# Storing an attention unit's output and softmax sums in five parts by heads in place of one store of 128 rows

## The chip, the cores and the metric

The kernel runs on one core of one Trainium2 chip. The metric is the device time of one execution in microseconds (us); lower is better. The engines are named as in the profile: PE is TensorE (matmuls; PEld its weight loads), DVE is VectorE, ACT is ScalarE, POOL is GpSimd, SP is SyncE. SPq and ACTq are the queues on which SP and ScalarE issue transfers (DMAs).

## The reference

The input x has 2048 rows of 640. It is normalized per row to xn, and the result is x + A(xn) + B(xn):

- A is attention with 32 heads of width 20 and a sliding window of 256: scores = q k^T / sqrt(20), masked so that a row sees itself and the 255 rows before it, softmax, times V, then times wo (640 x 640).
- B is a gated feed-forward of width 1728: gelu(xn w_gate) * (xn w_up), then times w_down.

## The kernel before, in words

Tokens are handled in NC = 4 chunks of C = 512. float32 products are made from a high and a low part (three matmuls each). The work has four stretches: normalization, transposes and the first projections; the attention loop, whose matmuls are interleaved with the remaining projections and a part of the gate and up products as filler; the remaining gate and up products; and the down and output projections.

**Units.** The attention loop (`attention`) runs over NU = 32 units. Unit u = 4 g + c is the group g of four heads and the chunk c. A unit has NS = 14 slots; in each slot some actions are emitted, and then RATE / NS filler matmuls (`pull_fill`). `defer(n, fn)` puts an action n slots later; `tick` runs what is due.

For a unit, in the order of time:

- `load_stack` (line 473, DMA at L482) brings the queries and keys of unit u + 3 from DRAM (`qd`, `kd`) into `qs` (three buffers) and `ks` (four buffers): six transfers each, of 20, 40 or 60 rows of 2 KB. The keys are asked for in slot KSLOT = 9, the queries in slot 12. They may start only when the matmuls that read the old content (L572) are done.
- `max_pair` (matmuls L507 into `ps_m`, row maxima by VectorE at L517) runs about one and a half units ahead of the exponentials. The first pair of unit u + 3 is emitted in slot 5 of unit u + 1.
- `max_end` (line 531) turns the maxima by a matmul (L534), copies them to `mr` (L536, ScalarE), and ScalarE itself issues the transfer `qs<-mr` (L537), which adds two rows to the queries. It is an entry in ScalarE's queue like any other, ahead of the activations behind it.
- `exp_piece` makes the scores (L572 into `ps_e`, two banks) and the exponentials (L574, ScalarE) into `P`; `clear` (L587, L590) sets masked ends to zero on POOL.
- `av_unit` (line 593), at the start of the next unit, multiplies P by V (L615 into two banks `ps_o`). V has a column of ones at each head's end, so that row 20 of each head's 32 rows holds the softmax sum. ScalarE copies one bank to `ob` (L621) and the other over a piece of P (L622); `join` (L625, three slots later) adds the second to the first on POOL; `store` (L628, five slots later) writes `ob` to DRAM. `ob` has one buffer: the next unit's copy at L621 waits for the store to have landed.

In `ob`, partition 32 j + d holds head 4 g + j: rows d = 0 to 19 are the output, row 20 is the sum, rows 21 to 31 are not used. In DRAM, `od[c]` (line 89) has 32 x 32 rows of 512, row 32 d + h for head h; `sd[c]` is the view of its rows 640 to 671, the sums. The later readers are L1085 (the sums), L1097 to L1108 (the outputs are divided by the sums and written back) and L1166 and L1169 (the outputs as operands of the last projection); they use rows 0 to 671 only.

**Who sets the order.** In the attention loop the order of PE, ACT, DVE and POOL is that of the program (`manual_schedule`, MANUAL and Pool). SP's order is not written out: the compiler's planner puts SP's transfers in order by when they become ready in its own model of time, and by program order among those. SP also issues the stores of projected queries and keys (`save_qk`, L268, from `pt`, made by POOL at L259), weight loads (L234, L637, L294), partial sums of x (L755, from `tx`, POOL) and hidden activations (L689).

Of the kernel before, what the change touches and what calls it, by code (L numbers as in the profile page):

```python
# [9 lines left out]
F32 = mybir.dt.float32  # L10
# [7 lines left out]
S, D, H, DH = 2048, 640, 32, 20  # L18
DF = 1728
C = 512  # L20
NC = S // C
# [46 lines left out]
def block_kernel(ctx, tc, x, wqk, wv, wgu, wdo, wdl, out):  # L68
    nc = tc.nc

    const = ctx.enter_context(tc.tile_pool(name="const", bufs=1))
    dram = ctx.enter_context(tc.tile_pool(name="dram", bufs=1, space=DRAM))
# [13 lines left out]

    qd = [dram.tile([NG, 3, 4 * DH, C], BF, name=f"qd{c}") for c in range(NC)]
    kd = [dram.tile([NG, 3, 4 * DH, C], BF, name=f"kd{c}") for c in range(NC)]
    od = [dram.tile([32 * H, C], F32, name=f"od{c}") for c in range(NC)]
    sd = [t[D:D + H] for t in od]  # L90
    td = [{i: dram.tile([128, 2, C], F32, name=f"td{p}{i}") for i in (1, 2, 3, 4)} for p in range(NC // 2)]
    wtd = [dram.tile([128, 4, HD], F32, name=f"wtd{q}") if q not in OWN else None for q in range(NQD)]
    rd = [dram.tile([H, C], F32, name=f"rd{c}") for c in range(NC)]
# [125 lines left out]
    def defer(n, fn, *a):  # L219
        if now[0] is None:  # L220
            fn(*a)
        else:
            at(now[0] + n, fn, *a)
# [315 lines left out]
    def pieces(c):  # L539
        b = 4 * c  # L540
        X = [(b, 0, 0, 384)] + ([(b - 2, 384, 0, 128)] if c else [])
        Y = [(b + 1, 0, 128, 384), (b + 3, 384, 384, 128)]
        Z = ([(b - 1, 0, 0, 256)] if c else []) + [(b + 2, 256, 256, 256)]
        return X, Z, Y
# [48 lines left out]
    def av_unit(u):  # L593
        g, c = divmod(u, NC)
        v = vtiles[g]
        os = [psx.tile([128, C], F32, name="ps_o", tag="ex") for _ in range(2)]
        place = {kb - 4 * c: (pts[u, bi], col, q0) for bi, bank in enumerate(pieces(c)) for kb, col, q0, n in bank}

        def half(d, r):
            i = 2 * d + r  # L600
            return d, r, max(0, 64 * i), min(C, 64 * i + 320)

        steps_ = [((0, 0), (0, 1)), ((2, 0), (-1, 1)), ((-1, 0), (2, 1)), ((1, 0), (1, 1)),
                  ((3, 0), (-2, 1)), ((-2, 0), (3, 1))]
        todo = [half(*x) for pair in steps_ for x in pair if x[0] in place]
        begun_, left = set(), [sum(t[1] == r for t in todo) for r in range(2)]
        for d, r, qa, qb in todo:
            pt, col, q0 = place[d]
            kb = 4 * c + d
            assert (id(v), kb) in done, (u, kb)  # L610
            left[r] -= 1
            rows = slice(64 * r, 64 * r + 64)
            for j in range(4):
                w0_ = kb * 84 + 21 * j
                nc.tensor.matmul(os[r][32 * j:32 * j + 32, qa:qb], v[rows, w0_:w0_ + 32],  # L615
                                 pt[rows, j, col + qa - q0:col + qb - q0], start=r not in begun_,
                                 stop=not left[r], skip_group_check=True, tile_position=(64 * r, 32 * j))
            begun_.add(r)
        ob, oc = ap.tile([128, C], F32, name="ob", tag="ob", bufs=1), pts[u, 2][:, 0]
        lo = 0 if c else 64  # L620
        nc.scalar.activation(ob, os[0], AF.Copy)  # L621
        nc.scalar.activation(oc[:, lo:], os[1][:, lo:], AF.Copy)  # L622

        def join():
            nc.gpsimd.tensor_tensor(out=ob[:, lo:], in0=ob[:, lo:], in1=oc[:, lo:], op=OP.add)  # L625

        def store():
            nc.sync.dma_start(od[c].rearrange("(d h) t -> h d t", h=H)[4 * g:4 * g + 4], ob)  # L628

        defer(3, join)  # L630
        defer(5, store)

    def load_gu(f):
# [892 lines left out]
```

## Time and profile before

| What | us |
|---|---|
| Time of three runs: median, lowest, highest | 1047.0, 1046.81, 1047.27 |
| The profiled execution's own time | 1046.35 |
| Its span, first to last instruction | 1044.6 |
| PE, DVE, ACT, POOL busy | 1034.0, 741.1, 527.6, 385.9 |
| First and last issue of the store at L628 | 106.4, 548.2 |
| DMA traffic | 161.60 MB in 102276 packets |

The profile is of one execution; its times count from the start of the span. A row of a timeline has the start, the length, the engine, the line, the operation, and out<-in tiles with a count; in brackets stands the idle time before it and what ended that. A row of the chain has start, length and what. "DMA od<-ob" in the chain is the time from a transfer's issue to its landing. A row of the waits has who waited for whom, the total, how often, and the longest. A row of a tile's instructions has min/median/max in ns, and first and last start in us.

### The profile page before, as it was taken

The numbers are of one execution on the slowest core, as the hardware profiler recorded it, in microseconds if no ns is written. First come the engines' busy times: TensorE is split into PE (matmuls) and PEld (weight loads), VectorE is DVE, ScalarE is ACT, GpSimd is POOL, SyncE is SP. The second block draws the span as 40 slices with busy tenths as digits, with TensorE's granted clock in tenths as the row PEclk, the third lists the DMA queues.
The fourth block names the chain that finished last, engine by engine and source line by source line (L and its number), as shares of the span: only waits on it lengthen the run. The fifth ranks groups of instructions, "written<-read, shape, count | busy, mean of one in ns | idle before, by whom it ended". The sixth has DMA issues, their size and how long they took to land.

```text
span 1044.6 us, 25328 instructions
## 1 busy us (share of the span) xinstructions
PE 1034.0 (99%) x9393; PEld 834.9 (80%) x9393; DVE 741.1 (71%) x2018; ACT 527.6 (51%) x1120; POOL 385.9 (37%) x623
## 2 busy tenths in 40 slices
PE   9999999999999999999999999999999999999998
PEld 8887666666787666666678888888888999999998
DVE  7755666676656576777736788775556888888887
ACT  4534767667666666666676232223224554433332
POOL 5122778888666787667470111101110000000000
PEclk9999999999999999999999999999999999999999
DMA  5552356655533464434225575663217874433333
GB/s 211 179 162 78 115 169 175 183 170 163 160 105 107 131 177 145 139 106 154 64 85 197 177 251 206 253 244 111 78 56 254 267 248 137 137 126 121 119 121 106
DMA packets 102276, 161.60 MB, mean 155 GB/s; under 512 B 12892, under 2 KB 53980, under 8 KB 102152
## 3 DMA queue, kind: packets, MB, share of 16 engines
q1 hardware_dynamic: 99768, 153.82, 45.9%
q10 hardware_dynamic: 2384, 6.16, 1.7%
q8 instruction: 74, 1.21, 0.5%
q14 instruction: 50, 0.41, 0.1%
HBM read 101.78 MB, written 57.80 MB: 153 GB/s over the span
## 4 chain that ended last, share of the span: by engine, by line
PE 89%; DVE 4%; POOL 2%; DMA 2%; issue 1%; ACT 1%; SPq 0%; DVEq 0%; POOLq 0%; ACTq 0%
PE ps_g L970 23%; PE ps L1242 23%; PE ps_d L108 18%; PE ps_e L572 7%; PE ps_v L108 7%; PE ps_o L615 5%; PE ps_m L507 4%; DVE junk L517 2%; PE ps_g L108 1%; DMA od<-ob 1%; PE ps_d L356 1%; POOL tx L751 0%; PE ps_t L185 0%; DMA qs<-qd 0%; ACT P L574 0%
## 5 line engine op out<-in xcount | busy, mean ns | idle before, releaser
L517 DVE CUSTOM_DVE_ANT_0 junk<-ps_m,mask 128x320 bf16<-128x320 f32 (+2 forms) x512 | 242.5, 474 | 130.5 <-PE ps_m L507 72.7
L574 ACT ACTIVATE P<-ps_e 128x512 f32<-128x512 f32 (+2 forms) x384 | 198.6, 571 | 68.5 <-PE ps_e L572 67.8
L1242 PE MATMUL ps<-wb,at 128*128 128x320 f32 x999 | 155.9, 309 | 0.0
L1242 PEld LDWEIGHTS ps<-wb,at 128*128 128x128 f32 x999 | 148.9, 188 | 0.2
L587 POOL TENSOR_SCALAR_AFFINE_SELECT P<-P 128x256 f32<-128x256 f32 (+1 forms) x192 | 95.2, 498 | 72.5 <-ACT P L574 69.0
L572 PE MATMUL ps_e<-qs,ks 124*128 124x128 bf16 (+2 forms) x704 | 118.6, 278 | 0.5 <-ACT P L574 0.3
L108 PE MATMUL ps_d<-xh,wqh 128*128 128x512 f32 x310 | 99.0, 422 | 0.2 <-ACT xh L193 0.2
L108 PE MATMUL ps_d<-xl,wqh 128*128 128x512 f32 x310 | 98.5, 421 | 0.0
L108 PE MATMUL ps_d<-xh,wql 128*128 128x512 f32 x310 | 97.6, 418 | 0.0
L101 POOL TENSOR_TENSOR wql<-wr,wqh 128x640 fp32r<-128x640 f32 x12 | 19.2, 1607 | 195.4 <-PE ps_g L970 150.8
L572 PEld LDWEIGHTS <-ks 124*128 124x128 bf16 x704 | 49.5, 98 | 49.8 <-issue 35.6
L1242 PE MATMUL ps<-wt,at 128*128 128x320 f32 x552 | 88.9, 309 | 0.0
L1242 PEld LDWEIGHTS ps<-wt,at 128*128 128x128 f32 x552 | 82.9, 188 | 0.1
L590 POOL TENSOR_SCALAR_AFFINE_SELECT P<-P 128x512 f32<-128x512 f32 (+1 forms) x144 | 76.9, 542 | 16.3 <-ACT P L574 16.3
L1196 ACT ACTIVATE at<-ss 128x512 fp32r<-128x512 f32 x59 | 37.2, 631 | 82.4 <-DVE ss L1075 82.4
L615 PE MATMUL ps_o<-P,v 64*32 64x320 f32 (+4 forms) x2816 | 74.2, 347 | 0.0
L259 POOL TENSOR_TENSOR pt<-r,pt 128x512 bf16<-128x512 f32 x40 | 46.8, 1171 | 67.4 <-ACT pt L255 67.4
L507 PE MATMUL ps_m<-ks,qs 60*64 60x320 bf16 (+3 forms) x1472 | 65.4, 260 | 4.0 <-DVE mx L517 1.5
L615 PEld LDWEIGHTS ps_o<-P,v 64*32 64x32 f32 x2816 | 50.8, 106 | 21.5 <-issue 0.9
L507 PEld LDWEIGHTS <-qs 60*64 60x64 bf16 x1472 | 29.5, 105 | 44.5 <-issue 37.7
L108 PEld LDWEIGHTS ps_d<-xh,wqh 128*128 128x128 f32 x310 | 56.0, 189 | 10.5 <-issue 1.6
L108 PEld LDWEIGHTS ps_d<-xh,wql 128*128 128x128 f32 x310 | 56.0, 189 | 10.2 <-issue 1.1
(195 smaller groups left out, 1966.6 us busy)
## 6 DMA issues: line engine op xcount, KB each, us to landing
hd<-he SPq DMA_DIRECT2D x50, 256.0 KB
hr<-hd SPq DMA_DIRECT2D x48, 256.0 KB
wr<-wgu SPq DMA_DIRECT2D x27, 320.0 KB
od<-ob SPq DMA_DIRECT2D x32, 256.0 KB
qs<-qd SPq DMA_DIRECT2D x64, 120.0 KB
ks<-kd SPq DMA_DIRECT2D x64, 120.0 KB
xi<-x SPq DMA_DIRECT2D x16, 320.0 KB
qs<-qd SPq DMA_DIRECT2D x64, 80.0 KB
```

The source lines that it names most:

```text
L108: nc.tensor.matmul(ps, a(k), b(k), start=n == 0, stop=n == 3 * nk - 1)
L259: nc.gpsimd.tensor_tensor(out=pt[:, l, :], in0=r, in1=pt[:, 1, :], op=OP.subtract)
L507: nc.tensor.matmul(ps[64 * h:64 * h + 64, col:col + w], q[rows, j, q0:q0 + 64], ks_, start=True, stop=True, tile_position=(64 * r, 64 * h))
L517: nc.vector.tensor_tensor_reduce(out=junk[:, 0:n], in0=ps[:, 320 - n:320], in1=mask[:, 320 - n:320], scale=1.0, scalar=NEG, op0=OP.add, op ...
L572: nc.tensor.matmul(ps[:, col:col + n], k[0:QROWS, j, kc:kc + 128], q[0:QROWS, j, q0:q0 + n], start=True, stop=True)
L574: nc.scalar.activation(pt[:, j, lo:hi], ps[:, lo:hi], AF.Exp, scale=SCALE)
L587: nc.gpsimd.affine_select(out=a, in_=a, pattern=[[0, n], [1, 128]], compare_op=OP.is_ge, fill=0.0, base=0, channel_multiplier=-1)
L590: nc.gpsimd.affine_select(out=a, in_=a, pattern=[[0, n], [-1, 128]], compare_op=OP.is_ge, fill=0.0, base=-1, channel_multiplier=1)
L615: nc.tensor.matmul(os[r][32 * j:32 * j + 32, qa:qb], v[rows, w0_:w0_ + 32], pt[rows, j, col + qa - q0:col + qb - q0], start=r not in begun ...
L970: nc.tensor.matmul(ps, i, j, start=first and n == 0, stop=n == len(work) - 1, skip_group_check=True)
L1196: nc.scalar.activation(hi[:, 3:7], s, AF.Copy)
L1242: nc.tensor.matmul(ps[bank][:, 0:HD], *work[bank][j], start=bank not in begun, stop=final[p, bank] == n and j == len(work[bank]) - 1, skip ...
```

## The change

`od[c]` shrinks from 1024 to 640 rows (the unused rows go), and the sums get a tensor of their own, `sd[c]`, of 32 rows. `store` writes, for each of the four heads, 20 rows of 512 floats (40 KB), and then the four rows of sums (partitions 20, 52, 84 and 116; 8 KB). So a unit has five transfers with 168 KB in all, in place of one with 256 KB. The readers stay as they are.

```diff
-    od = [dram.tile([32 * H, C], F32, name=f"od{c}") for c in range(NC)]
-    sd = [t[D:D + H] for t in od]
+    od = [dram.tile([D, C], F32, name=f"od{c}") for c in range(NC)]
+    sd = [dram.tile([H, C], F32, name=f"sd{c}") for c in range(NC)]
...
         def store():
-            nc.sync.dma_start(od[c].rearrange("(d h) t -> h d t", h=H)[4 * g:4 * g + 4], ob)
+            for j in range(4):
+                nc.sync.dma_start(od[c].rearrange("(d h) t -> h d t", h=H)[4 * g + j], ob[32 * j:32 * j + DH, :])
+            nc.sync.dma_start(sd[c][4 * g:4 * g + 4, :], ob[DH::32, :])
```

## The prediction

> **What bounds the kernel now.** I read the page's first and fourth parts first, then the stretches, then the waits of TensorE and of the DMA queue, then the rows of single units.
>
> ```profile
> span 1044.6 us, 25328 instructions
> PE 1034.0 (99%) x9393; PEld 834.9 (80%) x9393; DVE 741.1 (71%) x2018; ACT 527.6 (51%) x1120; POOL 385.9 (37%) x623
> PE 89%; DVE 4%; POOL 2%; DMA 2%; issue 1%; ACT 1%; SPq 0%; DVEq 0%; POOLq 0%; ACTq 0%
> ```
>
> TensorE is busy for 1034.0 of 1044.6 us and makes up 89% of the chain that ended last. A change to a store can therefore gain only where TensorE now stands still, and costs only where it makes TensorE stand still. The store L628 runs from 106.4 to 548.2 us (its row is below), so I cut the span there; the columns are the length, then PE, PEld, DVE, ACT and POOL busy, the clock, the DMA share and GB/s.
>
> ```profile
> 104.00:300.00 196.00, 193.89 (x2565) 131.29 (x2561) 129.95 (x487) 133.50 (x289) 155.99 (x262) 1.00 0.54 159
> 300.00:546.00 246.00, 244.31 (x3304) 167.61 (x3302) 159.61 (x580) 162.66 (x356) 168.38 (x287) 1.00 0.40 120
> ```
>
> In these stretches TensorE stands idle for 196.00 - 193.89 = 2.1 us and 246.00 - 244.31 = 1.7 us. So 3.8 us is the most that the visible idle time could give back, and the granted clock is 1.00 throughout. Who waits for what there:
>
> ```profile
> SPq L482 <- DMA od<-ob: 26.3, 16, 3.4
> SPq L268 <- DMA od<-ob: 10.4, 3, 3.9
> ...
> PEld L507 <- DMA qs<-qd: 2.2, 5, 0.7
> ...
> PE ps_m L507 <- DMA qs<-qd: 0.9, 3, 0.5
> ```
>
> Columns: total, times, longest. The store's landing holds up the DMA queue of SyncE (SP) for 26.3 + 10.4 = 36.7 us; TensorE's own waits on the loads behind it are small, 0.9 us, with 2.2 us more on its weight loads, which partly lie under matmuls. Why the landing holds a queue is seen in one unit. The first two rows are of the chain, the others of the timelines of SP and ACT.
>
> ```profile
> 138.53 7.20 DMA od<-ob
> 145.75 2.92 DMA ks<-kd
> ```
>
> ```profile
> 138.53 0.52 SPq L628 DMA_DIRECT2D od<-ob  x1
> 139.10 0.47 SPq L234 DMA_DIRECT2D wr<-wqk  x1
> 139.67 6.39 SPq L482 DMA_DIRECT2D ks<-kd  x6
> 146.60 1.03 SPq L482 DMA_DIRECT2D qs<-qd  x3
> 147.74 2.11 SPq L268 DMA_DIRECT2D qd<-pt  x3
> 149.96 1.06 SPq L482 DMA_DIRECT2D qs<-qd  x3
> 151.12 1.33 SPq L268 DMA_DIRECT2D kd<-pt  x3
> 152.55 0.50 SPq L755 DMA_DIRECT2D td<-tx  x1
> ```
>
> ```profile
> 140.22 0.62 ACTq L537 DMA_DIRECT2D qs<-mr  x1
> ```
>
> The store lands at 138.53 + 7.20 = 145.73, and the sixth ks load starts at 145.75. Between them seven transfers went off: wr, five ks, and qs<-mr from ScalarE's queue. The transfer eight places after the store waits for the store. I read this as a ring of eight places that SP and ScalarE share: each transfer waits until the one eight places before it has landed. Eight units later the same count fits:
>
> ```profile
> 253.41 0.52 SPq L628 DMA_DIRECT2D od<-ob  x1
> 253.98 0.46 SPq L637 DMA_DIRECT2D wr<-wgu  x1
> 254.54 1.22 SPq L482 DMA_DIRECT2D ks<-kd  x3
> 256.83 4.60 SPq L268 DMA_DIRECT2D qd<-pt  x3
> ```
>
> ```profile
> 255.90 0.65 ACTq L537 DMA_DIRECT2D qs<-mr  x1
> ```
>
> One wr, three ks, two qd and one qs<-mr make seven; the third qd stands waiting inside the 4.60 us, which three issues without a wait would fill to about 1.3.
>
> **The change part by part.** *Issue on SP.* One issue of 256 KB goes; four of 20 rows (40 KB) and one of 4 rows (8 KB) come.
>
> ```profile
> L628 SPq DMA_DIRECT2D od<-ob x32: 514/531/609, 106.4 to 548.2; - x32
> ...
> L482 SPq DMA_DIRECT2D qs<-qd x192: 272/328/1522, 44.0 to 501.3; - x192
> ...
> L454 SPq DMA_DIRECT2D ks<-ones x8: 577/577/758, 15.2 to 19.8; - x8
> ```
>
> min/median/max in ns. The qs loads have 20, 40 or 60 rows of 2 KB, the ks<-ones rows are four of 2 KB. So the five cost 4 x 0.33 + 0.58 = 1.9 us and, with gaps of 0.05 as between the rows above, about 2.15 us instead of 0.53: **+1.6 us per unit**, 51 us over 32 units, all on SP. In the unit above, the rows from 138.53 to 153.05 hold 21 issues of SP; at 0.33 to 0.53 each with gaps these are 8 to 12 us of 14.6, and over 3 us is the wait from the fifth ks to 145.75. So 1.6 us fits where that wait was. In the units after 300 us SP also waits for engines, so the cost lies in idle time there. Bounds per part: nothing, if every part replaces waiting, and 0.58 us, the four-row price.
>
> *Landing.* The store takes 7.20 us. Nearest rows for a part, loads of 20 to 60 rows:
>
> ```profile
> 250.69 2.30 DMA qs<-qd
> ...
> 265.29 2.46 DMA qs<-qd
> ```
>
> I take 2.4 us per part; 7.20 is the upper bound and 2.0 the lower (a little under the two rows, as a part moves no more than a third of what the 60-row load does). The parts overlap, so the last one lands 4 x 0.4 + 2.4 = 4.0 to 4.5 us after the first issue, some 3 us before the present store, and the wait 36.7 us largely goes. The loads issued during the store are slow too: ks at 139.67 and its followers wait behind it. By the ring the loads of the next units land 1 to 2 us earlier in about ten units from 125 to 300 us: 3.5 us of wait less 1.6 us of issue.
>
> The 7.20 us stand first in the trace. The Trainium skill (DMA: Bandwidth & Descriptors, section "Why a DMA increments its semaphore by 16 and not by 1") explains them: a transfer uses as many of the 16 engines as divide the outermost dimension on both sides. By it the present store, four heads outermost in DRAM, uses 4 engines and a 20-row part 10; the long landing agrees with it, though no row here counts the engines. By it the parts also free the engines for the loads behind, which would make my 2.4 us an upper value.
>
> *What TensorE gets.* The row for which loads are late:
>
> ```profile
> 152.38 0.47 PE L507 MATMUL ps_m<-ks,qs 60*64 60x256 bf16 x15 [0.55 <-DMA qs<-qd]
> ...
> 267.88 0.47 PE L507 MATMUL ps_m<-ks,qs 60*64 60x256 bf16 x15 [0.23 <-DMA qs<-qd]
> ```
>
> The three TensorE waits of this kind are 0.9 us together; the weight-load waits count for half (1.1 us of 2.2), as they partly lie under matmuls. Gain **about 2.0 us** if the loads come early enough everywhere. In the unit of 152.38 the second half of qs is issued at 149.96 behind qd<-pt, which waits for POOL (155.99 busy of 196.00), so part of the 0.55 stays. I take 1.5 us; bounds 0 and 3.8 (all idle).
>
> *ScalarE.* The next unit's copy into ob (L621) must now wait for five landings, not one. That is one or two extra short semaphore instructions; the copy then waits for TensorE's ps_o anyway:
>
> ```profile
> ACT ob L621 <- PE ps_o L615: 62.3, 28, 3.5
> ```
>
> That is 62.3 / 28 = 2.2 us of cover in 28 of 32 units, and the last part lands earlier than the one store does. I cost the extra waits at nothing; without that cover they would be some 0.1 us a unit on ScalarE.
>
> *The ring seen from ScalarE.* qs<-mr is ScalarE's own transfer in the same ring, and in order on ScalarE's queue ahead of the exponentials. At 140.22 its place is six behind the store's. With four more transfers ahead of it, the one eight places back becomes the store's third part. That part is issued near 138.53 + 2 x 0.45 = 139.4 and lands near 141.8, while qs<-mr now goes at 140.22: a **new wait of about 1.6 us**. In another unit it stands closer:
>
> ```profile
> 183.30 0.56 SPq L628 DMA_DIRECT2D od<-ob  x1
> ```
>
> ```profile
> 184.19 0.65 ACTq L537 DMA_DIRECT2D qs<-mr  x1
> 184.30 0.57 ACT L574 ACTIVATE P<-ps_e 128x512 f32<-128x512 f32 x1
> 185.78 1.09 ACT L574 ACTIVATE P<-ps_e 128x512 f32<-128x512 f32 x2 [0.91 <-PE ps_e L572]
> ```
>
> Here ScalarE is idle for 0.91 us behind qs<-mr, so a wait of 1.6 us costs ScalarE 0.7. The store precedes qs<-mr by 1.7, 0.9 and 2.5 us in the three units quoted; I take eight such units before 300 us (an estimate from these): 8 x 1.6 = 13 us of waiting, less 8 x 0.9 of cover = 5.6 us on ScalarE. TensorE has two score banks to run ahead with, and loses only some of that. I take a sixth, 0.9 us, as ScalarE has 62 us idle (196.00 - 133.50) in this stretch to catch up; bounds 0 and 5.6, or 13 without the cover.
>
> *From 546 us on* the same bytes are read and the sums come from a tensor of their own, long after the last store at 548.2. Nothing changes there.
>
> **Sum.** 1046.35 us of the profiled run (1.75 over its span) - 1.5 + 0.9 = 1045.75; the median shown is 0.65 us above that run, so **1046.4 us**. By bounds alone: 1047.0 - 3.8 = 1043.2 to 1047.0 + 5.6 = 1052.6.
>
> **The rivals.** *All idle time that loads cause goes and ScalarE never waits.* For it: SP's order is the planner's, and with SP busier qs<-mr may be put right behind the parts, where the place eight back is an old transfer. Against: POOL's share in the late qs. Price: -2.0 us to -3.8; time about 1044.4.
>
> *The wait moves to ScalarE.* For it: the ring of eight and 140.22. Price: 5.6 us on ScalarE with all of it on TensorE, against a gain of 1.5: +4 us, 1051. It decides once the store's third part lands more than about 1 us after qs<-mr is ready, in eight or more units. This is the case on the slower side.
>
> *Parts wait for each other.* The parts' rows interleave in DRAM with a pitch of 32. If the compiler takes them as overlapping, each waits for the landing before: 4 x 2.4 = 9.6 us more of SP per unit, beside 8 to 12 us of issue in 14.6. That is at least 3 us over in each of twelve units: 36 us, about 1083. Nothing in the trace speaks for it. The Trainium skill (DMA: Bandwidth & Descriptors, section "Rules for kernel authors") speaks against the change: transfers under 64 KB are mostly overhead and should be merged. In this trace that overhead lands off TensorE.
>
> **How the numbers follow.** A measurement here tells about 0.2%, 2.1 us, from no change. Forecast (no more than that, 1044.9 to 1049.1): 0.45. All idle gone, 1044.4: 0.17. ScalarE's wait, 1051: 0.28. Serial parts, 0.04, and another order of SP's transfers that makes loads late, some 3 to 10 us, 0.06. Faster 0.17, same 0.45, slower 0.28 + 0.04 + 0.06 = 0.38. The range takes in the first three cases and most of the last: 1044.0 to 1053.0.
>
> **What would show it.** Right: no wait of SP on the od parts near 3 us, landings of 2 to 3 us, the 0.55 us before ps_m smaller, and TensorE's idle time in 104 to 300 us between 1 and 2.5 us. Wrong: ScalarE standing before L537 for over 1 us with ps_e waiting for P (the second rival); SP waiting between parts (the third); idle time of TensorE before ps_m larger than now, with the ks and qs loads issued later.

## The result and the profile after

The changed kernel takes **1044.7 us** (median of 15 runs, 1044.32 to 1046.1) beside 1047.09 us (15 runs of the kernel before, taken with them, 1045.32 to 1048.86). The ratio is 0.9979, 95% interval 0.9971 to 0.9986. Measured a second time, in another group of runs (told below), it is 0.9989, 0.9979 to 0.9999. So the change makes the kernel slightly faster, by 2.4 us at the medians of the first group and by 1.3 us at those of the second; the two intervals together reach from 0.1 to 3.0 us.

The page of the changed kernel first: span, busy time and the chain by engine.

```profile
span 1042.7 us, 25560 instructions
PE 1032.4 (99%) x9393; PEld 834.0 (80%) x9393; DVE 742.1 (71%) x2018; ACT 527.6 (51%) x1120; POOL 384.5 (37%) x623
PE 89%; DVE 3%; POOL 3%; DMA 1%; issue 1%; ACT 1%; SPq 0%; DVEq 0%; POOLq 0%; ACTq 0%
```

The span is 1.9 us shorter, and DMA's part of the chain falls from 2% to 1%; the links "DMA od<-ob" are gone from it. The same two stretches as in the prediction:

```profile
104.00:300.00 196.00, 194.93 (x2580) 132.93 (x2576) 131.93 (x494) 135.28 (x297) 156.90 (x265) 1.00 0.52 154
300.00:546.00 246.00, 244.29 (x3297) 167.39 (x3296) 160.25 (x575) 162.16 (x354) 167.58 (x285) 1.00 0.37 115
```

TensorE's idle time falls from 2.11 to 196.00 - 194.93 = 1.07 us in the first stretch and stays at 1.7 us in the second. All of the gain is made before 300 us. The starts of ps_o, once per unit, show it as well; of before, then of after:

```profile
145.32 0.98 PE L615 MATMUL ps_o<-P,v 64*32 64x320 f32 x24
160.46 0.77 PE L615 MATMUL ps_o<-P,v 64*32 64x320 f32 x16
...
275.35 0.96 PE L615 MATMUL ps_o<-P,v 64*32 64x320 f32 x24
```

```profile
145.32 0.99 PE L615 MATMUL ps_o<-P,v 64*32 64x320 f32 x24
159.30 1.93 PE L615 MATMUL ps_o<-P,v 64*32 64x320 f32 x64
...
273.20 1.93 PE L615 MATMUL ps_o<-P,v 64*32 64x320 f32 x64
```

Both kernels start the same unit at 145.32; the next one starts 15.14 us later before and 13.98 us later after. At the unit of 275.35 the changed kernel leads by 2.15 us. From there on the units of the two are equally long to within 0.04 us. Five units between 145 and 273 us are shorter, by 1.14, 0.25, 0.51, 0.46 and 0.60 us, about 3.0 together; one, from 215.91, is 0.77 us longer. The lead is more than the 1.04 us by which the idle time fell. I read the rest as time that had been counted as busy, in matmuls spread out while their weights were waited for: the weight loads' 2.2 us of waiting for queries at L507 have no row any more, and all rows of these loads that name a transfer fall from 4.1 to 2.4 us (rows for od and kd<-pt have grown from 0.4 us each to 1.3 and 1.1). No run shows that share by itself.

The waits of SP's queue, then those of TensorE:

```profile
SPq L482 <- PE ps_e L572: 16.7, 25, 2.3
SPq L482 <- DMA qs<-mr: 3.0, 2, 1.7
```

```profile
PE ps_m L507 <- DMA qs<-qd: 0.5, 1, 0.5
```

No row of SP names od any more, where it was 36.7 us; of what is left of the ring, the 3.0 us for qs<-mr are the largest row. Of TensorE's three waits for queries one is left. The new issues on SP, min/median/max in ns:

```profile
L629 SPq DMA_DIRECT2D od<-ob x128: 272/323/1504, 106.5 to 547.2; - x128
L630 SPq DMA_DIRECT2D sd<-ob x32: 490/505/569, 107.9 to 547.6; - x32
```

That is 4 x 0.32 + 0.51 = 1.8 us a unit without gaps. Now the unit that the prediction went through, SP's timeline and then ScalarE's transfer:

```profile
138.62 1.41 SPq L629 DMA_DIRECT2D od<-ob  x4
140.08 0.50 SPq L630 DMA_DIRECT2D sd<-ob  x1
140.70 3.04 SPq L482 DMA_DIRECT2D ks<-kd  x6
143.84 1.38 SPq L268 DMA_DIRECT2D qd<-pt  x3
145.32 2.18 SPq L482 DMA_DIRECT2D qs<-qd  x6
```

```profile
140.17 0.62 ACTq L537 DMA_DIRECT2D qs<-mr  x1
```

Two things are to be seen. The four parts go out in 1.41 us, one behind another, so none waits for the landing before it. And SP's order is another one: wr, which stood between store and keys, is gone from there, and qs<-mr at 140.17 follows the parts at once, ahead of all six keys. The transfer eight places back of it is one from before the store, already landed. The keys need 3.04 us in place of 6.39.

From each transfer's issue and completion records in the trace I worked out how long the landings take (medians): the old store 6.5 us, a 20-row part 1.55 us, the sums 1.7 us. The keys of the attention loop also land sooner: in 3.5 us before (the longest 8.5), in 2.4 us after (4.6).

The one wait that is left, at TensorE and what SP did ahead of it:

```profile
223.07 0.47 PE L507 MATMUL ps_m<-ks,qs 60*64 60x256 bf16 x15 [0.47 <-DMA qs<-qd]
```

```profile
213.60 0.93 SPq L234 DMA_DIRECT2D wr<-wqk  x2
214.58 2.24 SPq L482 DMA_DIRECT2D ks<-kd  x6
217.69 3.04 SPq L482 DMA_DIRECT2D qs<-qd  x6
```

```profile
SPq L482 <- DMA wr<-wqk: 1.8, 2, 1.0
```

In this unit, the one that became 0.77 us longer, the queries go out from 217.69 to 220.7; by the trace's records the fifth lands at 222.94 and TensorE starts at 223.07. Nothing of the store lies between, but the ring does: the first two queries stand eight places behind the two weight loads wr of 320 KB. These land at 217.62 and 218.94, and the two queries are issued at 217.69 and 218.96. SP's 1.8 us of waiting are both in this unit, and the second weight load is a link of the chain, with 4.85 us. So what is left of the wait for queries is the old mechanism with another long transfer.

### The profile page after: what moved, and what is told of

Same layout as the page of the kernel before. It is cut to its first block, busy times and chain, and to the rows that moved or that the text cites. A ratio compares the mean times of both kernels' runs of the same rounds, so it can differ in the third digit from the quotient of the medians.

```text
span 1042.7 us, 25560 instructions
## 1 busy us (share of the span) xinstructions
PE 1032.4 (99%) x9393; PEld 834.0 (80%) x9393; DVE 742.1 (71%) x2018; ACT 527.6 (51%) x1120; POOL 384.5 (37%) x623
## 4 chain that ended last, share of the span: by engine, by line
PE 89%; DVE 3%; POOL 3%; DMA 1%; issue 1%; ACT 1%; SPq 0%; DVEq 0%; POOLq 0%; ACTq 0%
PE ps_g L972 23%; PE ps L1244 23%; PE ps_d L108 18%; PE ps_e L572 7%; PE ps_v L108 7%; PE ps_o L615 5%; PE ps_m L507 4%; DVE junk L517 2%; PE ps_g L108 1%; POOL pt L259 1%; POOL P L587 1%; POOL P L590 1%; PE ps_d L356 1%; PE ps_t L185 0%; DMA kd<-pt 0%
## 5 line engine op out<-in xcount | busy, mean ns | idle before, releaser
L507 PE MATMUL ps_m<-ks,qs 60*64 60x320 bf16 (+3 forms) x1472 | 64.7, 260 | 3.3 <-DVE mx L517 1.5
L507 PEld LDWEIGHTS <-qs 60*64 60x64 bf16 x1472 | 29.1, 105 | 43.7 <-issue 38.5
```

The costliest lines, as they stand in the source:

```text
L507: nc.tensor.matmul(ps[64 * h:64 * h + 64, col:col + w], q[rows, j, q0:q0 + 64], ks_, start=True, stop=True, tile_position=(64 * r, 64 * h))
```

## The experiments

Theory: the gain comes from the store's **landing**. While the old store takes 6.5 us, the loads behind it in the ring are held and land late; whatever shortens the landing brings the gain. Rivals: the gain comes from the fewer bytes (168 KB, not 256 KB), from the number of parts, or from the other order of SP. The first four kernels ran on one chip beside 16 runs of the kernel before (median 1046.53).

**Four transfers of all 32 rows, in the old layout.** The kernel before with

```diff
-            nc.sync.dma_start(od[c].rearrange("(d h) t -> h d t", h=H)[4 * g:4 * g + 4], ob)
+            for j in range(4):
+                nc.sync.dma_start(od[c].rearrange("(d h) t -> h d t", h=H)[4 * g + j], ob[32 * j:32 * j + 32, :])
```

> The DRAM layout of before stays; the store is four transfers of 32 rows (64 KB each, sums and unused rows included), one per head. All 256 KB are still written. Landing theory (the gain is the short landing, whatever the bytes): parts land in about 1.6 to 2 us, and the time is that of the changed kernel, 1044.4 to 1045.2. Bytes theory (the gain is 88 KB less per unit): no gain, 1046.6 to 1047.4. Order theory (the gain is that the planner, with more transfers in the ring, moves ScalarE's qs<-mr away from late ones): gain as in the changed kernel.

Measured: 1043.6 us (1043.48 to 1044.83), ratio 0.997, 0.9959 to 0.9981. The first stretch:

```profile
104.00:300.00 196.00, 195.29 (x2580) 133.29 (x2581) 131.54 (x494) 135.69 (x297) 157.55 (x265) 1.00 0.55 161
```

The idle time is 0.71 us, less than with the change, though all 256 KB are stored; a part lands in 1.7 us. So fewer bytes are not the cause, and neither are the addresses: these four transfers write the same rows of DRAM as the old store.

**One store of 128 consecutive rows.** The later readers are left as they are, so they take other rows for outputs and sums than those that they need, and the result is not the reference's; their work is the same. The kernel before with

```diff
-            nc.sync.dma_start(od[c].rearrange("(d h) t -> h d t", h=H)[4 * g:4 * g + 4], ob)
+            nc.sync.dma_start(od[c][128 * g:128 * g + 128], ob)
```

> One store of 128 rows as before, 256 KB, one issue, but into 128 consecutive rows of DRAM (the readers are left as they are, so the output rows and sums that they read are in another order than the reference's: the result is not the reference's). Landing theory: the store lands in 2 to 3 us instead of 6.5 to 7.2, and the time falls at least as far as in the changed kernel, 1043.8 to 1044.8, as SP is spared 1.6 us per unit. Bytes theory: no gain, 1047. Order theory: the same number of transfers, so no gain, 1046.6 to 1047.4.

Measured: 1043.53 us (1043.32 to 1044.63), ratio 0.9971, 0.9959 to 0.9983. Its first stretch and its store:

```profile
104.00:300.00 196.00, 195.39 (x2585) 133.47 (x2589) 132.00 (x494) 135.75 (x297) 157.68 (x267) 1.00 0.53 162
```

```profile
L628 SPq DMA_DIRECT2D od<-ob x32: 319/338/397, 106.3 to 545.1; - x32
```

One transfer of the same 256 KB, in the same place of the program, lands in 2.1 us, is issued in 0.34 us in place of 0.53, and brings the idle time to 0.61 us. The orders of PE, VectorE, ScalarE and POOL are unchanged, and SP's is nearly so. So neither the splitting nor the new order is what brings the gain. What this store shares with the four parts of 32 rows is its form: the outermost dimension is 128 or 32 rows, and not four heads. The trace's records show how that bears on it: the old store, four heads outermost, is completed by 5 counts, a 20-row part by 11, a 32-row part and this store by 16. The Trainium skill (DMA: Bandwidth & Descriptors, section "Why a DMA increments its semaphore by 16 and not by 1") has each engine that takes part post one count and, where they are fewer than 16, the issuing sequencer write the rest at once. I take that rest as one record more; qs<-mr, with two rows, has 3 records. Then 5, 11 and 16 counts are 4, 10 and 16 engines, the numbers that divide the outermost dimensions. 4 and 16 engines go with 6.5 and 2.1 us for the same bytes.

**Four parts by columns.** Each part keeps all four heads outermost, and so the old store's form:

```diff
-            nc.sync.dma_start(od[c].rearrange("(d h) t -> h d t", h=H)[4 * g:4 * g + 4], ob)
+            for a in range(4):
+                nc.sync.dma_start(od[c].rearrange("(d h) t -> h d t", h=H)[4 * g:4 * g + 4, :, 128 * a:128 * a + 128],
+                                  ob[:, 128 * a:128 * a + 128])
```

> The layout of before; the store is cut into four transfers by columns (128 of 512 each), each over all 128 rows, so each has the four heads outermost in DRAM as the one store had. 256 KB are written. Landing theory: the last slice lands 6 to 8 us after the first issue, the loads behind stay slow, SP pays about 1.5 us more per unit: no gain, 1047 to 1050. Bytes theory: no gain, 1047. Order theory: four transfers as in the first kernel of this group, so the same gain, 1044.4 to 1045.2.

Measured: 1049.27 us (1048.54 to 1050.11), ratio 1.0024, 1.0014 to 1.0033: slower than before, with as many parts of the same size as the first kernel had. A slice lands in 2.9 us (up to 5.5), a 32-row part in 1.7 (the slice's rows are 512 bytes and not 2 KB, so the form is not all that differs). What TensorE waits for, and one such place, first SP, then ScalarE, then TensorE:

```profile
104.00:300.00 196.00, 192.90 (x2551) 130.71 (x2548) 130.44 (x486) 132.59 (x289) 154.92 (x260) 1.00 0.53 158
300.00:546.00 246.00, 243.27 (x3226) 166.36 (x3233) 157.64 (x577) 162.09 (x356) 165.41 (x284) 1.00 0.39 120
```

```profile
PE ps_e L572 <- ACT P L574: 2.4, 4, 1.0
```

```profile
367.52 2.21 SPq L629 DMA_DIRECT2D od<-ob  x4
369.83 0.93 SPq L268 DMA_DIRECT2D qd<-pt  x2
370.86 3.38 SPq L482 DMA_DIRECT2D ks<-kd  x6
```

```profile
370.60 1.05 ACT L574 ACTIVATE P<-ps_e 128x512 f32<-128x512 f32 x2
372.51 0.65 ACTq L537 DMA_DIRECT2D qs<-mr  x1
373.26 1.08 ACT L574 ACTIVATE P<-ps_e 128x512 f32<-128x512 f32 x2 [1.62 <-POOL P L587]
```

```profile
373.91 0.87 PE L572 MATMUL ps_e<-qs,ks 124*128 124x128 bf16 x4 [0.69 <-ACT P L574]
```

This is the prediction's second rival at work. Back from qs<-mr at 372.51, in the order of the ring, stand four keys, two qd and two slices, so the third of the four slices is the one eight places back; by the trace's records it lands at 372.43. ScalarE is done with its exponentials at 371.65, stands until then, spends 0.65 us on the issue, and is idle for 1.62 us in all (the POOL named in the brackets is only the wait that ended last by the profile). TensorE waits 0.69 us for the exponential. All four of TensorE's waits of this kind, 2.4 us together, come within 3 us behind such a qs<-mr. By the records qs<-mr had to wait for the transfer eight places back in nine units; with the change in none. In five of the nine that transfer is a slice, in the others a weight load or a key; two of the four waits, 1.02 and 0.69 us, stand behind slices. No row of TensorE's own waits names a load any more, so the slices, too, let the queries come in time: the loss is on ScalarE's side. The idle time in both stretches is 3.10 + 2.73 = 5.8 us, 2.0 more than before.

**Nine parts.** The changed kernel with each head's 20 rows as two transfers:

```diff
-                nc.sync.dma_start(od[c].rearrange("(d h) t -> h d t", h=H)[4 * g + j], ob[32 * j:32 * j + DH, :])
+                for i in (0, 10):
+                    nc.sync.dma_start(od[c].rearrange("(d h) t -> h d t", h=H)[4 * g + j, i:i + 10],
+                                      ob[32 * j + i:32 * j + i + 10, :])
```

> The changed kernel with each head's 20 rows in two transfers of 10, so nine transfers per unit in place of five. This doubles the suspected cost, SP's issue and the places in the ring. If SP's issue has slack: within 0.5 us of the changed kernel, 1044.2 to 1045.4. If issue is what keeps the changed kernel from the full gain: 1.4 us more of SP per unit shows in late loads in the units up to 300 us, 1046 to 1049. If ScalarE's transfer gets a young part eight places ahead: ScalarE waits up to 1 us before qs<-mr in some units.

Measured: 1050.89 us (1048.5 to 1052.87), ratio 1.0036, 1.0022 to 1.005. The parts land as fast as ever (1.5 us), and still:

```profile
PE ps_m L507 <- DMA qs<-qd: 3.1, 5, 0.9
```

```profile
166.74 3.24 SPq L630 DMA_DIRECT2D od<-ob  x8
170.02 0.54 SPq L632 DMA_DIRECT2D sd<-ob  x1
...
172.87 2.69 SPq L482 DMA_DIRECT2D ks<-kd  x6
```

```profile
SPq L482 <- PE ps_e L572: 3.9, 8, 1.7
```

The store now takes 3.8 us of SP, and the loads behind it are late. The last row is SP's wait until the scores have let go of a load's buffer: after the change 16.7 us, here 3.9. Before the change it was:

```profile
SPq L482 <- PE ps_e L572: 38.9, 33, 4.2
```

That wait is spare time which SP has ahead of the loads, and with nine parts little of it is left. I read this as SP's issue being the limit here, and near with five parts. Not all of the time is lost there: the last matmul of ps_o starts at 546.98 us in place of 543.23, 3.75 us later, and a wait of 1.45 us for DVE xr (L1269) comes at 840.32, of a kind that is met again below.

The next four kernels ran on one chip beside 17 runs of the kernel before (median 1047.22).

**The old store from GpSimd's queue.** To part the two ways in which a long landing can hurt, holding the ring or occupying the DMA engines, the kernel before issued its store by `nc.gpsimd.dma_start` in place of `nc.sync.dma_start`.

> The kernel before with its one store of 256 KB per unit unchanged, issued by GpSimd in place of SyncE. It keeps the long landing (6.5 us on the few engines that the old layout reaches) but no transfer of SyncE's eight-deep ring has to wait for it. If the gain comes from the ring alone (SyncE's 36.7 us of waits for the store, and the loads that they delay): SyncE's waits for od are gone, TensorE's idle time in 104 to 300 us falls from 2.1 to about 1 us, and the time is about 1045 us. If the gain comes from the engines that the store occupies while loads run: the idle time stays near 2 us and the time near 1046.5 us. A third outcome: issuing the store costs GpSimd more than it does SyncE and holds up the causal selects of P; then TensorE waits for P and the time is above 1047 us.

Measured: 1050.9 us (1048.8 to 1052.21), ratio 1.0035, 1.0022 to 1.0048. The store's time to landing, then SP's waits, ScalarE's and TensorE's:

```profile
DMA to landing us min/median/max: 5.8/7.4/8.7
```

```profile
SPq L482 <- DMA ks<-kd: 22.6, 14, 4.0
```

```profile
ACT ob L621 <- DMA od<-ob: 17.8, 6, 3.4
```

```profile
PE ps_n L534 <- DVE mx L517: 2.2, 1, 2.2
PE ps_e L572 <- ACT ob L621: 2.0, 4, 0.7
```

It doesn't part them cleanly. No row of TensorE's own waits names a load any more, and the unit from 145 us lasts 13.99 us, as with the change: that speaks for the ring. But keys now wait 22.6 us for earlier keys: keys land in 3.1 us (the longest 8.1), less than the 3.5 us of before and more than the 2.4 us with the change. So the transfer also slows what runs beside it. And time is lost elsewhere, not at the causal selects as the third outcome had it. GpSimd issues the store a little later, and its landing now comes after the next unit's ps_o is done, so ScalarE's copy into the single buffer ob waits for it, 17.8 us in six units, of which 2.0 reach TensorE. Another 2.2 us, in the profiled execution, are one VectorE instruction that took 4.97 us:

```profile
193.42 4.97 DVE L526 TENSOR_SCALAR nm<-mx 128x16 bf16<-128x16 f32 x1
```

Its median is 0.175 us. GpSimd worked without a gap from 189.2 us on, and the instruction ended when GpSimd came to its transfer at 198.32; why it was held that long is not shown. Unit by unit the trace says more. Of the first thirteen units, from 102 us on, eleven are as long here as with the one store of 128 rows, to within 0.02 us, four of those that the change shortened among them. The other two are longer by 0.45 and 3.25 us and hold waits of TensorE of 0.29 us in the one, 0.63 and 2.24 us in the other. So a store that still lands in 7.4 us costs those four units nothing once it is out of the ring (SP is also spared its issue). That speaks for the ring as the way by which the long landing cost time; a share of the engines is not seen there, and not excluded in the two other units.

**The changed kernel, the first experiment again, and one store with adapted readers.** These three are compared with one another. The third has the layout of the second experiment with wo's rows in the same order, and readers that pick the pieces of each head (their lines are left out here):

```diff
-    sd = [t[D:D + H] for t in od]
+    sd = [t.rearrange("(h d) t -> h d t", d=32)[:, DH] for t in od]
...
-            nc.sync.dma_start(od[c].rearrange("(d h) t -> h d t", h=H)[4 * g:4 * g + 4], ob)
+            nc.sync.dma_start(od[c][128 * g:128 * g + 128], ob)
...
-    wo = np.asarray(A_wo).reshape(H, DH, D).transpose(1, 0, 2).reshape(D, D)
+    wo = np.asarray(A_wo).reshape(H, 5, 4, D).transpose(1, 0, 2, 3).reshape(D, D)
```

> The changed kernel once more, beside the two others on the same chip. If the first comparison holds: 0.2 per cent below the kernel before, about 1044.5 us, and between the kernel before and the two other layouts.

> The four transfers of 32 rows once more, beside the changed kernel. If the fifth transfer and its place in SyncE's order cost the changed kernel about 1 us: 1043.5 us, about 1 us below the changed kernel. If the difference between the first comparisons was that of the jobs: within 0.3 us of it.

> One store of 128 rows per unit into 128 consecutive rows of DRAM, as in the run with one contiguous store, now with the readers adapted: the rows of wo are laid out in the same order, and each later load picks its four-element pieces of every head, some as several transfers in place of one. In the attention stretch it should show the same as that run: TensorE idle about 0.6 us in 104 to 300 us, and by that stretch alone 1043.5 us. The readers' transfers are more and spread over shorter runs of rows; if SyncE has room for them there, 1043.5 us; if they make the loads of the later stretches late, TensorE's idle time after 546 us rises and the time is 1045 us or more.

| Kernel | us, median (lowest to highest) | Ratio to before, 95% |
|---|---|---|
| five parts (the change) | 1045.91 (1044.35 to 1049.3) | 0.9989 (0.9979 to 0.9999) |
| four parts of 32 rows | 1043.45 (1043.4 to 1043.51) | 0.9962 (0.9951 to 0.9974) |
| one store by head rows | 1043.81 (1043.64 to 1044.18) | 0.9966 (0.9955 to 0.9978) |

The first stretch of the change's second profile and of the four parts; the one store has the same 195.39 us as the latter:

```profile
104.00:300.00 196.00, 194.87 (x2580) 132.95 (x2577) 131.93 (x494) 135.33 (x297) 156.97 (x265) 1.00 0.52 154
```

```profile
104.00:300.00 196.00, 195.39 (x2581) 133.46 (x2579) 131.91 (x494) 135.80 (x297) 157.66 (x266) 1.00 0.55 162
```

The changed kernel's attention repeats to within 0.1 us per unit in its second profile: idle 1.13 us, and again one wait of 0.5 us for queries in the unit from 215.9 us, which lasts 14.99 us here and 14.13 us in the kernel with one store. Its median is 1.4 us above the 1044.5 us expected. The four parts of 32 rows lie 2.5 us under it by the medians of this group (about 1 us was expected), and 1.1 us by those of the first two groups. About 1 us of that is seen in the attention stretch, 0.5 us of it as idle time. More lies far behind it, in the last projections, where the change's second profile has a wait that its first profile and those of the two other kernels do not show (the nine parts have it, 1.45 us):

```profile
836.06 14.31 PE L1244 MATMUL ps<-wb,at 128*128 128x320 f32 x96 [0.98 <-DVE xr L1267]
```

The executions of the two profiles took 1044.47 us without this wait and 1045.63 us with it. What brings it in one execution and not in another is not settled. It is a reason to give the change's gain as no closer than 1.3 to 2.4 us. The best versions are thus four parts of 32 rows and one store by head rows, 0.34 to 0.38% under the kernel before. Every run of either lies below every run of the change in this group; between themselves they differ by 0.36 us, which is too little to choose by.

## Why the prediction was right or wrong

The forecast was 1046.4 us, no more than 0.2% from before (1044.9 to 1049.1); measured were 1044.7 us, 0.2 us beyond that border on the fast side, and 1045.9 us, within it. Where the gain comes from was right: the store's long landing held SP's ring and made queries late. Two terms of the sum were wrong, both the same way: the gain came out at 2.15 us and not 1.5, and the cost on ScalarE at nothing and not 0.9. What happened is nearly the first rival, 1044.4 us with a chance of 0.17, and for the reason that stood there, qs<-mr right behind the parts. That 1046.4 us is off by no more than 1.7 us is in part luck: both terms are small, and the second group comes nearer to it at least in part by a wait far behind the attention loop, of which the sum knew nothing.

- **Issue on SP, +1.6 us a unit, in place of waiting.** Right: 1.41 + 0.50 us and two gaps in the unit at 138.62, 2.0 us against 0.53. It replaced the wait of 36.7 us and part of the spare time behind the scores (38.9 us before, 16.7 after). The nine parts show how near the bound was: four transfers more cost 5 to 6 us at the medians, 3.75 us of it in the attention loop by the profiles.
- **Landing, 2.4 us a part.** Too long: 1.55 us. The sentence that called 2.4 us an upper value, by the rule of the engines, was the better guide, and the forms of experiments one to three agree with that rule.
- **Gain on TensorE, 1.5 us of a possible 2.0.** Mis-sized. The changed kernel gains about 3.0 us in five units and gives 0.8 back in one, 2.15 us in all. I had discounted the 2.0 us because in the unit of 138.53 the second half of the queries stood behind qd<-pt, which waits for POOL. In that unit of the changed kernel all six go out from 145.32 to 147.5, where the last three were issued from 149.96 on. And the waits from which I took the 2.0 us hold less than the late loads cost, as the lead of the units against the idle time shows.
- **ScalarE's wait in the ring, +0.9 us.** This step failed. It took SP's order as given and put four more transfers between the old eighth place and qs<-mr. The planner set the parts and wr elsewhere, and qs<-mr came right behind the parts, with an old transfer in its eighth place; waits: none, where the kernel before has four. The prediction had named this as what speaks for its first rival. That the mechanism is real the four column slices show: nine such waits, five of them behind a slice, and 2.4 us at TensorE, where the second rival had 5.6.
- **The copy into ob, nothing.** Right: ScalarE's list has no wait for od, and its cover is still there.

```profile
ACT ob L621 <- PE ps_o L615: 61.7, 28, 3.5
```

  Without the cover, in the kernel that stores from GpSimd, it became 17.8 us.
- **Parts that wait for each other.** Did not happen: four issues in 1.41 us.
- **After 546 us, nothing.** Right for the code: the same work, and in the first profile the whole lead of 2 us is kept. The spread of the second group has its place there.
- **The rule against small transfers.** The Trainium skill (DMA: Bandwidth & Descriptors, section "Rules for kernel authors") has transfers under 64 KB merged. Against the old store it misleads here: 40 KB parts beat it, because the old store's form uses few engines. Among transfers that use their engines it agrees: one of 256 KB does what four of 64 KB do, with a fourth of the issues, five are 1.1 to 2.5 us behind, and nine cost 5 to 6 us more.

## What to carry to other kernels

Before splitting a slow transfer, look at its outermost dimension on both sides: the same 256 KB landed in 6.5 us with 4 outermost and in 2.1 us with 128, and that alone brought more than the five parts did. A landing hurts not only by its own length but by what stands eight transfers behind it, on the other engine's queue too; and where a planner sets the order, a step that argues from the old order has to be priced for the new one as well. When the slow store is mended, the next long transfer in the ring shows: here the weight loads, with 1.8 us. The spare time of the issuing engine is a budget of which its waits for buffers tell (38.9, 16.7, 3.9 us here): when it nears zero, more parts cost more than they free.

## What the runs showed that was not expected

- The parts also speed the loads next to them: keys land in 2.4 us where they took 3.5 beside the old store (medians of the attention loop).
- Issue has a price by form: 0.53 us for the old store and for a slice of it, 0.51 for four rows, 0.42 for 32 rows, 0.34 for 128 consecutive rows, 0.32 for 20 rows. The size of the transfer doesn't set it.
- One VectorE instruction of 0.175 us took 4.97 us beside a GpSimd that worked without a gap. The Trainium skill (SBUF — State Buffer, section "SBUF: two separate sides") has the two share a port pair by an exclusive lock that is held for the whole instruction. That fits a wait behind GpSimd, but no instruction of GpSimd in that time took more than 1.26 us, so one such hold does not make 4.97, and no run here tests it.
- Issued by GpSimd, the old store takes 0.71 us to issue in place of 0.53, and 7.4 us to land in place of 6.5. Another queue doesn't mend the form.
